# A fused attention, routed expert and feed-forward kernel: routing moved to a score tile's spare columns, first expert tile prepared on GpSimd

## The chip, the cores and the metric

One Trainium2 chip, one core. The metric is device time of one execution in microseconds (us); lower is better. The engines named below are TensorE (PE, with PEld for its weight loads), VectorE (DVE), ScalarE (ACT), GpSimd (POOL) and SyncE (SP), which issues most transfers.

## The reference

Three stages in a row, all in float32:

```python
# 1. attention, (B, H, S, D) = (2, 8, 576, 64)
q_rot, k_rot = rotate(q), rotate(k)
attn = softmax(q_rot @ k_rot.T / sqrt(D));  x = attn @ v      # -> (1152, 512)
# 2. eight experts, top 1
logits = x @ w_gate + modality_bias[modality_id]              # (1152, 8)
e_idx, gate_w = argmax(logits), max(softmax(logits))
out[e_idx == e] = gate_w * (relu(x @ w1[e]) @ w2[e])          # 512 -> 1024 -> 512
# 3. feed forward
h = out @ w_in;  y = (h * tanh(softplus(h))) @ w_out          # 512 -> 2048 -> 512
```

## The kernel before

Every product is made of matmuls on a rounded high part and a low part (value minus high part), so each operand has to be split: a copy to the high part, mostly on ACT, and a subtraction for the low part on DVE or POOL.

**Attention** goes over 16 heads in pairs. For each block of queries PE makes scores (`score`, L930), DVE their maximum (`smax`), ACT the exponential (`sexp`), PE transposes (`tr`), ACT and DVE split the transposed block (`t_hi`, `t_lo`), PE multiplies with v into the tile `avp` (`pv`), ACT copies that out (`f_evac`), PE turns it back and multiplies it with the router's weights in the same matmul (`f_mm`), and DVE divides by the softmax sum (`f_norm`, L1045). `f_norm` writes twice: the 64 columns of a head into `X`, the 8 logits of a head into `LG`. POOL prepares each head's q, k and v ahead of it (L884 to L925) and adds 1e-9 to the softmax sums (`f_rec`).

The order of the whole stage is worked out when the program is built, by `Plan` (L74): each operation has an engine, an estimated time, a key (about when it is due) and the operations it depends on; an engine takes the first operation by key that is ready within 0.05 us, else the one that is ready first. The result is a fixed order on each engine's queue, and an instruction at the head of a queue that is not ready in fact holds up all behind it. Streams (`Plan.add`) are generators whose steps are fitted in between. A step of an engine named in `low` is taken only into a gap that it fits.

**Routing** (`routing`, L307) is done once for each half of the tokens (b = 0 after head 7, b = 1 after head 15): logits, argmax, one matmul that counts tokens for each expert (L362, L363), the row of each token in a sorted scratch buffer, five indirect DMAs from POOL that scatter the rows of `X` there (L413), and a table of which expert and which 304 rows make each expert tile. The intermediates lie in PSUM in `rtile`, which for b = 0 is columns 320 to 511 of `avp`, the bank into which `pv` multiplies. Dependencies are kept tile by tile, so DVE's routing instructions and PE's `pv` wait for each other though they touch other columns.

**The expert stage** has two tiles for each half (`moe_tile`): (0,0), (0,1), (1,0), (1,1). A tile loads its rows (`load_rows`, L571), multiplies them by the gate (`moe_g`, L633, ACT), transposes them (`moe_x`, L650), and takes eight weight chunks (`load_chunk`, `split_chunk`, L588 and L593): four for the first layer, f = 0 to 7, two each, and four for the second, d = 0 to 3. For (0,0) the low parts of chunks 3 and 4 are made on DVE. After the half-0 table, SP reads the tile's registers (`tile_rows`), loads rows and two chunks, and ACT and POOL split these chunks in gaps of the last heads. PE's transposes of (0,0) come behind the attention's last matmul. Then the routing of half 1 runs on DVE, and `pump` puts as many PE steps of the expert tiles before each DVE step as `P["rq"]` says (0.45, 0.47, 0.2 us). Behind it stand nine more PE steps and then `n_extra = nc.values_load(nx)`, a register read on every engine of a value that the last routing instruction (L544) writes: PE cannot go on before it. The scatters of half 1 and the row loads of half 0 touch one scratch buffer, so whichever comes second waits for the other.

**The last stage** (from about 293 us) decodes the feed-forward weights on DVE and runs the two products.

Of the kernel before, what the change touches and what calls it, by code (L numbers as in the profile page):

```python
# [28 lines left out]
XC = DM  # L29
# [39 lines left out]

LOW = ("act", "dve", "pool")  # L70
# [3 lines left out]
class Plan:  # L74
# [72 lines left out]
    def add(self, gen, ready, low=(), end=None):  # L147
        st = {"gen": gen, "ready": ready, "low": low, "end": end}
        st["next"] = next(gen, None)
        self.streams.append(st)  # L150
# [18 lines left out]
    def run(self):  # L169
# [3 lines left out]
        while any(self.todo.values()):  # L173
            best = None
            for e in self.todo:
# [10 lines left out]
                for st in self.streams:  # L186
                    if st["next"][0] != e:
                        continue
                    t = self.start(st)
                    if c is None or t + (st["next"][1] - P["slack"] if e in st["low"] else 0.0) <= c[0]:  # L190
                        c = (t, 0, st)
# [19 lines left out]
def moe_kernel(ctx: ExitStack, tc: tile.TileContext, aps, out):  # L211
# [16 lines left out]
    LG = [xp.tile([128, 5, H, NE], F32, name=f"LG{b}") for b in range(B)]  # L228
# [76 lines left out]
    scat, nxs, tes, tms = [], [], [], []  # L305

    def routing(b, bank):  # L307
# [4 lines left out]
        def near(sh, nm):  # L312
# [19 lines left out]
            out=lg, in_=LG[b].rearrange("p j h e -> p j e h"),  # L332
# [12 lines left out]
        val = near(sh, "val")  # L345
# [27 lines left out]
        if side:  # L373
            V.memset(base[:, 0:1], 0.0)
        yield "dve", 0.2, True
        if side:
            scan()
            room[0] = 90
            pz = near([128, n], "pz")
            V.tensor_tensor(out=pz, in0=ps[:, n:2 * n], in1=base[:, 0:n], op=ALU.add)  # L380
            V.tensor_copy(cnt[:, 0:n], ps[:, 0:n])
        else:
            V.tensor_copy(cnt, ps[:, 0:2 * n])
        sm8 = near([128, 5], "sm8")
        yield "dve", 0.12, True
        V.tensor_reduce(out=sm8, in_=ex, axis=AX.X, op=ALU.add)
        yield "dve", 0.12, True
        V.tensor_scalar(out=sm8, in0=sm8, scalar1=1e-9, scalar2=None, op0=ALU.add)
        yield "dve", 0.12, True
        V.reciprocal(out=X[b][:, :, XC + 1], in_=sm8)  # L390
        if not side:
            yield "dve", 0.12, True
            V.memset(base[:, 0:1], 0.0)
            yield "dve", 0.12, True
            scan()
        if not side:
            pz = t([128, n], "pz")
            yield "dve", 0.12, True
            V.tensor_tensor(out=pz, in0=cnt[:, n:2 * n], in1=base[:, 0:n], op=ALU.add)
        yield "dve", 0.12, True  # L400
# [68 lines left out]
        if side:  # L469
            room[0] = 0  # L470
# [95 lines left out]
    def load_rows(k):  # L566
# [3 lines left out]
        for i, (r0, rn) in enumerate(TCH):  # L570
            ld = nc.sync.dma_start(out=t[:rn, i], in_=scratch[ds(r["c"] + r0, rn), :])  # L571
            if k != "x":
                after_scatters(ld)
# [1030 lines left out]
```

## Time and profile before

| | us |
|---|---|
| median of three runs | 524.64 |
| lowest, highest | 520.6, 524.78 |
| the profiled execution | 524.0 |
| its span, first to last instruction | 522.3 |

| engine | busy us of the span | share |
|---|---|---|
| PE | 481.5 | 92% |
| DVE | 408.8 | 78% |
| POOL | 365.1 | 70% |
| ACT | 332.8 | 64% |

The mean granted clock of PE is 0.98. Matmuls overlap in the profile, so PE counts as busy also where it is not at its best rate; the number of matmuls in a stretch says more. Attention ends near 177 us, the expert stage near 293 us.

### The profile page before, as it was taken

How to read it: one execution, taken by the hardware profiler on the slowest of the kernel's cores; microseconds unless marked ns; L12 is line 12 of the kernel's file. 1: busy time of each engine (PE TensorE's matmuls, PEld its weight loads, DVE VectorE, ACT ScalarE, POOL GpSimd, SP SyncE). 2: the span in 40 equal slices, each digit the busy share in tenths (PEclk: the TensorE clock that was granted, in tenths of full speed). 3: DMA queues.
4: the chain of work that ended last, by engine and by line, in shares of the span. 5: the costliest groups of instructions: out<-in, count | busy, mean ns of one | idle time of the engine just before them, and what ended most of it. 6: DMA issues, size and time to landing. Idle time of an engine off the chain costs nothing.

```text
span 522.3 us, 9180 instructions
## 1 busy us (share of the span) xinstructions
PE 481.5 (92%) x3152; PEld 445.3 (85%) x3152; DVE 408.8 (78%) x622; ACT 332.8 (64%) x748; POOL 365.1 (70%) x359
## 2 busy tenths in 40 slices
PE   2699999998899879998999988899999899999995
PEld 1689999987799778997999987688999789999894
DVE  6478989888989583852467999999999967877773
ACT  2378788766688745454464475666666568776773
POOL 4869999989680535774867566677777558977664
PEclk9969999999999998999999999999999899999999
DMA  6568885866654277594776522022220000100001
GB/s 210 144 160 213 230 226 146 208 191 187 166 107 133 80 266 279 216 315 163 246 249 215 228 82 80 2 80 82 81 82 1 1 1 40 41 21 1 2 2 80
DMA packets 24132, 68.67 MB, mean 131 GB/s; under 512 B 5522, under 2 KB 9810, under 8 KB 22034
## 3 DMA queue, kind: packets, MB, share of 16 engines
q1 hardware_dynamic: 21794, 62.70, 39.7%
q0 software_dynamic: 1456, 4.74, 2.4%
q10 hardware_dynamic: 832, 0.61, 0.4%
q8 instruction: 26, 0.43, 0.3%
q14 instruction: 24, 0.20, 0.1%
HBM read 48.77 MB, written 5.99 MB: 105 GB/s over the span
## 4 chain that ended last, share of the span: by engine, by line
PE 35%; DVE 13%; issue 2%; ACT 2%; POOL 0%; POOLq 0%
PE h L1411 13%; PE o L1468 13%; PE mm L684 9%; DVE ta L1433 6%; DVE yl L1359 2%; DVE wc L1259 2%; DVE wc L1264 1%; DVE ta L1434 1%; DVE wc L1254 1%; ACT w2h L1394 0%; PE mm L650 0%; POOL out_dram L1478 0%; ACT ta L1423 0%; POOLq L1600 0%; ACT ta L1422 0%
## 5 line engine op out<-in xcount | busy, mean ns | idle before, releaser
L1433 DVE RECIPROCAL ta<-ta 128x320 f32<-128x320 f32 (+1 forms) x64 | 124.7, 1948 | 21.9 <-ACT ta L1426 19.7
L1451 POOL TENSOR_TENSOR g<-ta,g 128x320 fp32r<-128x320 f32 (+1 forms) x63 | 60.1, 954 | 61.4 <-issue 29.0
L1468 PE MATMUL o<-w2h,g 128*128 128x512 f32 x288 | 100.4, 396 | 0.0
L1395 POOL TENSOR_TENSOR w2l<-wc,w2h 128x512 fp32r<-128x512 f32 x64 | 85.9, 1364 | 3.4 <-ACT w2h L1394 3.4
L1411 PE MATMUL h<-yh,w2h 128*128 128x320 f32 (+1 forms) x256 | 76.8, 300 | 6.2 <-DVE ta L1434 6.2
L1411 PE MATMUL h<-yl,w2h 128*128 128x320 f32 (+1 forms) x256 | 76.3, 298 | 1.1 <-DVE yl L1359 1.1
L1411 PE MATMUL h<-yh,w2l 128*128 128x320 f32 (+1 forms) x256 | 76.5, 299 | 0.0
L939 PE MATMUL sc<-sk,sq 128*128 128x288 f32 (+1 forms) x320 | 60.7, 322 | 15.1 <-ACT sk L870 9.3
L956 ACT ACTIVATE pexp<-sc,nm 128x576 f32<-128x576 f32 x72 | 53.3, 740 | 23.5 <-DVE nm L949 17.9
L989 ACT ACTIVATE ph<-pt 128x512 fp32r<-128x512 f32 (+2 forms) x112 | 54.5, 509 | 16.8 <-PE pt L969 15.8
L949 DVE TENSOR_REDUCE nm<-sc 128x1 f32<-128x576 f32 x72 | 53.6, 751 | 12.8 <-PE sc L939 11.2
L1468 PEld LDWEIGHTS o<-w2h,g 128*128 128x128 f32 x288 | 54.1, 189 | 11.0 <-POOL g L1451 1.1
L939 PEld LDWEIGHTS sc<-sk,sq 128*128 128x128 f32 (+1 forms) x320 | 48.7, 198 | 17.0 <-ACT sk L870 9.3
L1411 PEld LDWEIGHTS h<-yh,w2h 128*128 128x128 f32 x256 | 48.6, 190 | 11.1 <-DVE ta L1434 7.8
L969 PE MATMUL pt<-ident,pexp 128*128 128x128 f32 (+1 forms) x360 | 55.7, 282 | 2.1 <-DVE rs L1034 1.6
L1468 PE MATMUL o<-w2l,g 128*128 128x512 f32 x144 | 56.8, 394 | 0.0
L1010 PE MATMUL av<-ph,vhl 128*128 128x256 f32 (+1 forms) x160 | 52.0, 340 | 2.4 <-DVE av L331 0.5
L1445 ACT ACTIVATE g<-ta 128x320 fp32r<-128x320 f32 (+1 forms) x64 | 27.9, 436 | 41.3 <-DVE ta L1434 41.2
L995 DVE TENSOR_TENSOR pl<-pt,ph 128x512 fp32r<-128x512 f32 (+1 forms) x80 | 49.3, 629 | 3.2 <-ACT ph L989 2.5
L1411 PEld LDWEIGHTS h<-yl,w2h 128*128 128x128 f32 x256 | 48.6, 190 | 3.6 <-DVE yl L1359 1.4
L1411 PEld LDWEIGHTS h<-yh,w2l 128*128 128x128 f32 x256 | 48.7, 190 | 0.1
L969 PEld LDWEIGHTS pt<-ident,pexp 128*128 128x128 f32 (+1 forms) x360 | 43.9, 141 | 4.0 <-issue 2.1
(445 smaller groups left out, 1222.1 us busy)
## 6 DMA issues: line engine op xcount, KB each, us to landing
wr<-in_wio_dram SPq DMA_DIRECT2D x16, 1024.0 KB, 5.0
xs<-in_qk_dram SPq DMA_DIRECT2D x15, 576.0 KB, 5.3
sk<-ab SPq DMA_DIRECT2D x30, 288.0 KB, 3.8
sq<-ab SPq DMA_DIRECT2D x30, 144.0 KB, 2.3
vraw<-in_v_dram SPq DMA_DIRECT2D x16, 160.0 KB, 3.9
scratch<-zero SPq DMA_DIRECT2D x12, 96.8 KB, 4.4
tabs<-in_rope_dram SPq DMA_DIRECT2D x2, 288.0 KB, 4.8
xs<-in_qk_dram ACTq DMA_DIRECT2D x2, 288.0 KB, 4.5
```

The source lines that it names most:

```text
L939: nc.tensor.matmul(t[:m, hf, :NC2], lhsT=sq[:, c:c + m], rhs=sk[:, z, hf * NC2:(hf + 1) * NC2], start=(z == 0), stop=(z == 1),)
L949: nc.vector.tensor_reduce(out=nm[n, j], in_=sc[n, j][:, :, :NC2], axis=AX.XY, op=ALU.max, negate=True)
L956: nc.scalar.activation(out=pe, in_=sc.pop((n, j))[:, :, :NC2], func=AF.Exp, bias=nm.pop((n, j)), accum_out=st[n, hf][:, i:i + 1],)
L969: nc.tensor.transpose(out=t[:kn, o:o + 128], in_=pexp[n, j][:, k0:k0 + kn], identity=ident)
L989: nc.scalar.activation(out=block(ph, n, hf, kts, slice(0, kn)), in_=psum(n, hf, kts, kn), func=AF.Copy)
L995: nc.vector.tensor_tensor(out=block(pl, n, hf, kts, slice(0, 128)) if kn == 128 else block(ph, n, hf, kts, slice(64, 128)), in0=psum(n, hf ...
L1010: nc.tensor.matmul(av[n, hf][:, :u.nq], lhsT=vhl[n][:, kt].rearrange("p a d -> p (a d)"), rhs=src[:, kt, u.at:u.at + u.nq], start=(kt == 0 ...
L1395: nc.gpsimd.tensor_tensor(out=lo[:, cs], in0=w[:, cs], in1=hi[:, cs].bitcast(F32), op=ALU.subtract)
L1411: nc.tensor.matmul(ps[:, :w], lhsT=wt[:, c], rhs=m[g, i][:, c], start=(n == 0), stop=(n == 11))
L1433: nc.vector.reciprocal(out=ta, in_=ta)
L1451: eng.tensor_tensor(out=gt[q][1][:, o:o + w], in0=tas.pop((q, i))[:, :w], in1=gt[q][0][:, o:o + w].bitcast(F32), op=ALU.subtract,)
L1468: nc.tensor.matmul(acc[g, t], lhsT=a[:, s], rhs=b, start=(f == 0 and z == 0), stop=(f == FC2 - 1 and z == 2),)
```

## The change

1. `X` takes the logits too: a head has 72 columns in it (`XC = H * XW`), `LG` is gone, and `f_norm` writes once. Scattered rows and loaded rows are 580 columns wide instead of 516.
2. The score tiles become two fixed tiles `scp`. The routing of half 0 keeps its first intermediates in the spare columns of one of them, and a gate (`is_spare`) lets its steps be placed only between that tile's maximum and its next scores. The part behind the counting matmul works in the matmul's own bank and in SBUF, in one step; 1e-9 is added on ACT.
3. The scatters of half 0 become a stream that takes only gaps on POOL. The table of half 0 becomes a stream of its own, in SBUF, that starts after the last head's low part (`plo`) on POOL. Rows are loaded when both are done.
4. Scatters of one half no longer wait for row loads of the other, nor the loads for them.
5. For tile (0,0) POOL makes the gates and the high and low parts of chunks 0 to 2, as soon as the rows are there; PE's transposes become twelve matmuls in four operations `xt` of the plan, due at key `XK` = 162, with ACT and DVE splitting them. Softmax sums of the last two heads go to ACT.

```diff
-XC = DM
+XC = H * XW
+XK = 10.0 * B * H + 2.0
...
-    LG = [xp.tile([128, 5, H, NE], F32, name=f"LG{b}") for b in range(B)]
...
-        if side:
-            scan()
-            room[0] = 90
-            pz = near([128, n], "pz")
+        yield "dve", 0.8, True
+        V.tensor_tensor_scan(
+            out=base[:, 1:], data0=ps[:, 0:n], data1=zero[:, :n],
+            initial=0.0, op0=ALU.add, op1=ALU.add,
+        )
+        pz = ps[:, 2 * n:3 * n]
...
-        V.tensor_scalar(out=sm8, in0=sm8, scalar1=1e-9, scalar2=None, op0=ALU.add)
+        yield "act", 0.2, True
+        nc.scalar.activation(out=sm8, in_=sm8, func=AF.Copy, bias=1e-9)
...
+        if b:
+            yield from scatters()
+        else:
+            cur["scatters"] = scatters()
+            yield "mark", 0.0, False
+            side = False
...
-    def after_scatters(ld):
-        for o in scat:
+    def after_scatters(ld, b):
+        for o in scat[1 - b]:
+            tc.declare_no_dep(ld.ins, o, reason="rows of the other half")
+        for o in scat[b]:
...
-        yield "act", 0.95, False
-        nc.scalar.activation(out=hi, in_=w, func=AF.Copy)
+        if k == (0, 0) and i < 3:
+            yield "pool", 1.3, False
+            nc.gpsimd.tensor_scalar(
+                out=hi, in0=w, scalar1=1.0, scalar2=0.0, op0=ALU.mult, op1=ALU.add
+            )
...
-            yield "act", 0.5, i == 2
+            yield ("pool", 0.7, False) if k == (0, 0) else ("act", 0.5, i == 2)
...
+        def is_spare(t):
+            return spare[0] == 1 or spare[0] == 2 and t >= spare[1]
...
-            for dst, c0, c1 in (
-                (X[b][:, j0:j0 + m, h * D:(h + 1) * D], 0, D),
-                (LG[b][:, j0:j0 + m, h], D, XW),
-            ):
+            nc.vector.tensor_tensor(
+                out=X[b][:, j0:j0 + m, h * XW:(h + 1) * XW], in0=x[:, :m],
+                in1=r[:, :m, None].to_broadcast([128, m, XW]), op=ALU.mult,
+            )
...
+    def ahead(done):
+        yield from feed.loads(5)
+        yield from moe_g(k0)
+        x_new(k0)
+        done()
+        yield from feed.splits(3)
...
+        for c in range(KC):
+            op = lambda n, e, d, fn, dep, **kw: plan.op((n, c), e, d, XK, fn, deps=dep, **kw)
+            op("xt", "pe", 0.35, lambda c=c: xt(c), ["gate0"], take=[("ring", ("x", c))])
+            op("xh", "act", 0.4, lambda c=c: x_hi(k0, c, xps[c]), [("xt", c)])
+            op("xl", "dve", 0.44, lambda c=c: x_lo(k0, c, xps[c]), [("xh", c)],
+               give=[("ring", ("x", c))])
...
-            plan.add(until_pe(gen0), plan.now + 2.2, low=LOW)
+            plan.add(begin, plan.now + 2.2, low=("act", "dve"))
...
+        plan.op("scatter", "sp", 0.0, z, scatter, deps=["rt_row"])
+        plan.op("table", "sp", 0.0, z, table, deps=["rt_row", ("plo", B * H - 1)])
         plan.op(
             "rows", "sp", 2.2, z, weights,
-            deps=["rt_end", ("stack", B * H - 1), ("vload", B * H - 1)],
+            deps=["rt_end", "rt_sc", ("stack", B * H - 1), ("vload", B * H - 1)],
         )
```

## Rows read from the trace of the kernel before

**Rows 1.** Stretches of attention: length, busy (x instructions) per engine, clock, DMA, GB/s.

```profile
80.00:100.00 20.00, 20.00 (x163) 19.53 (x162) 17.91 (x40) 16.32 (x43) 18.86 (x21) 1.00 0.68 175
100.00:120.00 20.00, 18.61 (x138) 16.54 (x137) 16.36 (x49) 13.47 (x34) 17.34 (x22) 1.00 0.72 196
120.00:140.00 20.00, 16.09 (x115) 13.92 (x114) 17.44 (x50) 12.34 (x32) 17.78 (x22) 1.00 0.70 186
140.00:160.00 20.00, 19.96 (x159) 19.13 (x159) 18.01 (x42) 16.16 (x41) 11.69 (x15) 1.00 0.49 105
```

**Rows 2.** Waits between 100 and 140 us: total us, times, longest.

```profile
ACT pexp L956 <- DVE base L374: 1.7, 1, 1.7
...
PEld av L1010 <- DVE av L331: 0.8, 1, 0.8
```

**Rows 3.** Timeline of POOL: start, us, line, operation, [idle before <-releaser].

```profile
111.60 1.42 POOL L890 TENSOR_TENSOR xs<-xs 128x576 f32<-128x576 f32 x1
114.15 1.20 POOL L413 DMA_INDIRECT scratch<-X,row  x1 [1.12 <-DVE row L410]
...
120.85 0.67 POOL L896 TENSOR_SCALAR ab<-xs 128x576 fp32r<-128x576 f32 x1
...
134.14 2.65 POOL L884 TENSOR_TENSOR xs<-xs,tabs 128x1152 f32<-128x1152 f32 x1
...
150.86 1.42 POOL L905 TENSOR_TENSOR ab<-xs,ab 128x576 fp32r<-128x576 f32 x1
...
180.44 2.37 POOL L593 TENSOR_TENSOR wlo(0, 0)_2_2682<-wraw(0, 0)_2_2554,whi(0, 0)_2_2680 128x1024 fp32r<-128x1024 f32 x1 [3.36 <-ACT whi(0, 0)_2_2680 L588]
190.33 1.08 POOL L413 DMA_INDIRECT scratch<-X,row  x1 [7.52 <-DMA xrow(0, 1)_2757<-scratch]
```

**Rows 4.** Timeline of DVE, the same columns.

```profile
134.40 2.41 DVE L519 CAST tbl<-te 1x4 int32<-1x4 f32 x1
...
176.91 0.29 DVE L1054 TENSOR_TENSOR X<-xo,rs 128x128 f32<-128x128 f32 x1 [1.80 <-PE xo L1040]
...
177.77 0.47 DVE L657 TENSOR_TENSOR xl(0, 0)_2605<-mm,xh(0, 0)_2604 128x304 fp32r<-128x304 f32 x1 [0.49 <-ACT xh(0, 0)_2604 L655]
...
187.46 0.15 DVE L410 TENSOR_SCALAR row<-rt 128x5 int32<-128x5 f32 x1
...
195.35 0.14 DVE L544 TENSOR_TENSOR nxi<-nx,nx 1x1 int32<-1x1 f32 x1
```

**Rows 5.** Timeline of PE from the end of attention.

```profile
176.20 0.67 PE L1040 MATMUL xo<-mov,avt 128*128 128x72 f32 x4 [0.47 <-ACT avt L1019]
176.70 2.24 PE L650 MATMUL mm<-ident,xrow(0, 0)_2385 128*128 128x128 f32 x12
...
181.39 0.41 PE L362 MATMUL mm<-oh,ones 128*128 128x40 f32 x2 [0.69 <-DVE base L374]
...
192.64 0.30 PE L684 MATMUL mm<-xl(0, 0)_2605,whi(0, 0)_3_2734 128*128 128x304 f32 x1
192.78 0.30 PE L684 MATMUL mm<-xh(0, 0)_2604,wlo(0, 0)_3_2736 128*128 128x304 f32 x1
196.38 0.38 PE L684 MATMUL mm<-xh(0, 0)_2604,whi(0, 0)_3_2734 128*128 128x304 f32 x1 [3.29 <-DVE hl(0, 0)_2677 L709]
```

**Rows 6.** Stretches behind that wait, columns as in rows 1.

```profile
196.00:200.00 4.00, 3.62 (x19) 3.65 (x20) 2.02 (x3) 0.42 (x1) 2.92 (x3) 0.73 0.73 220
200.00:204.00 4.00, 4.00 (x27) 4.00 (x25) 0.74 (x1) 2.33 (x4) 1.19 (x1) 0.85 0.98 393
```

**Rows 7.** SP's register reads of the table (ns min/median/max), and its row loads.

```profile
L549 SPq TENSOR_LOAD <-tbl x4: 271/509/981, 154.1 to 195.6; - x4
...
158.32 1.48 SPq L571 DMA_DIRECT2D xrow(0, 0)_2385<-scratch  x3
```

**Rows 8.** Landing of the last row load of tile (0,0), us.

```profile
xrow(0, 0)_2385<-scratch SPq DMA_DIRECT2D x1, 96.8 KB, 3.6
```

**Rows 9.** POOL's one-input form: busy us, mean ns, idle before.

```profile
L896 POOL TENSOR_SCALAR ab<-xs 128x576 fp32r<-128x576 f32 x15 | 10.1, 674 | 2.0 <-DMA sk<-ab 1.1
```

More of the change, by code (lines that the diff above doesn't have):

```diff
@@ L145, in take, with add @@
                 self.slots[r].append(end + LAT[o[3]])
-    def add(self, gen, ready, low=(), end=None):
-        st = {"gen": gen, "ready": ready, "low": low, "end": end}
+    def add(self, gen, ready, low=(), end=None, gate=None):
+        st = {"gen": gen, "ready": ready, "low": low, "end": end, "gate": gate}
         st["next"] = next(gen, None)
@@ L189, in run @@
                     t = self.start(st)
+                    if st["gate"] and not st["gate"](t):
+                        continue
                     if c is None or t + (st["next"][1] - P["slack"] if e in st["low"] else 0.0) <= c[0]:
@@ L410, in routing, with scatters @@
         V.tensor_scalar(out=row, in0=pos, scalar1=s1, scalar2=o1, op0=ALU.mult, op1=ALU.add)
[L411 to L420 removed]
+        def scatters():
+            for j, (_, qn) in enumerate(QT):
+                yield "pool", 1.07, False
+                sc = nc.gpsimd.indirect_dma_start(
+                    out=scratch,
+                    out_offset=bass.IndirectOffsetOnAxis(ap=row[:qn, j:j + 1], axis=0),
+                    in_=X[b][:qn, j], in_offset=None,
+                )
+                for o in scat[0] + scat[1]:
+                    tc.declare_no_dep(sc.ins, o, reason="every token has a row of its own")
+                for o in early if b else ():
+                    tc.declare_no_dep(sc.ins, o, reason="rows of the other half")
+                scat[b].append(sc.ins)
+                nc.gpsimd.memset(spacer, 0.0)
+        if b:
[4 more added lines that the diff above has]
+            side = False
+        room[0] = 256
         ce = near([1, NE], "ce")
@@ L468, in routing @@
         s8 = [1, ns, NE]
[L469 to L470 removed]
+        room[0] = 0
         lt = near(s8, "lt")
@@ L1197, in hook, with until_mark, mark @@
         cur["rbank"] = lambda: bank("counts")
+        def until_mark():
+            for y in r0:
+                if y[0] == "mark":
+                    return
+                yield y
+        def mark(name):
+            return lambda t: plan.done.update({name: ("dve", t)})
         def start():
-            plan.add(until_pe(r0), plan.now, end=lambda t: plan.done.update(rt=("dve", t)))
+            plan.add(until_pe(r0), plan.now, end=mark("rt"), gate=cur["spare"])
         def rest():
             next(r0)
-            plan.add(r0, plan.now + 0.2, end=lambda t: plan.done.update(rt_end=("dve", t)))
+            plan.add(until_mark(), plan.now + 0.8, end=mark("rt_row"))
@@ new lines, in scatter, with table, xt @@
+        def scatter():
+            plan.add(cur["scatters"], plan.now, low=("pool",), end=mark("rt_sc"))
+        def table():
+            plan.add(r0, plan.now, end=mark("rt_end"))
+        begin = ahead(lambda: plan.done.update(gate0=("pool", plan.free["pool"])))
+        cur["begin"] = begin
+        xps = {}
+        def xt(c):
+            xps[c] = bank(f"x{c}")
+            x_tr(k0, c, xps[c])
+        for c in range(KC):
[4 more added lines that the diff above has]
+               give=[("ring", ("x", c))])
```

149 lines of the change are left out of this document (82 added, 67 removed).

## The prediction

> **What bounds the kernel now.** I read first the busy times by stretch of the attention [rows 1]. Where no routing runs, PE is busy throughout and gets 163 matmuls through in 20 us, 8.15 in a microsecond, while DVE and POOL are near 90%. From 100 to 140 us it does 138 and 115. At the former rate these 253 need 31.0 us: routing half 0 inside the attention costs 9.0 us, 3.1 of them up to 120 and 5.9 behind. The waits of that stretch say how [rows 2]: ACT's exponential stood 1.7 us for a routing instruction on DVE, and PE's product stood for the router's reduction into the bank they share. POOL's timeline shows another part [rows 3]: between the addition at 111.60 and the next preparation at 120.85 it only scatters (about 1.3 us a piece, five of them), so later heads' operands come some 7 us late.
>
> Then I read the timelines around the end of attention. PE goes from the last outputs (176.20) to twelve transposes of tile (0,0) (2.2 us) and its products [rows 5]; it waits 0.69 us for the argmax and stops at 192.92, until 196.38. The wait is put down to DVE, but the product at 196.38 needs nothing new: the instruction behind the nine steps is the register read of `nx`, which DVE writes at 195.49 [rows 4]. So DVE's routing chain, from the norm at 176.91 to 195.49 (18.6 us), sets this point, and the read takes 0.9 more. Behind the stop the granted clock falls to 0.73 and 0.85 of a stretch of 4 us [rows 6], between its levels of 1.2 and 2.4 GHz: 1.1 + 0.6 = 1.7 us lost. From there on the stages follow one another; I take a shift at this point to reach the end.
>
> **Routing half 0 (the gain).** The sum is made against the profiled execution, 524.0 us, 0.6 under the median. Of the 9.0 us the false waits on `avp` go, and the scatters no longer come before the heads' preparation. What stays is DVE's work: in the first part some 15 instructions, in the table some 18 of 0.15 us upward [rows 4], about 0.2 with their issue, 3.6 in all, into an engine busy 18.0 of 20 [rows 1]. Half of the first part's loss stays (1.5), and the table costs 2.0 where it now lies (from 147 us), the rest fitting into DVE's idle tenth: gain 9.0 - 3.5 = 5.5. Bounds: 9.0 if all of this is hidden; 9.0 - 3.1 - 3.6 = 2.3 if the first part stays and the table is paid whole. I take 5.5, since PE is the full engine in [rows 1]. One write instead of two in `f_norm` shortens DVE; PE's full rate hides it, so nothing. Wider rows: PE, DVE and ACT touch no more than before; transfers have slack, nothing.
>
> **Gates, chunks and transposes.** Price of a chunk on POOL: its low part 2.37 [rows 3], its high part at 0.674 for 576 columns [rows 9] 1.2 for 1024: 3.57. When do they start? The table starts behind the last `plo`, now 152.3 [rows 3], then 5.5 earlier, 146.8. Its 18 instructions alternate with attention's (18.0 us for 42 instructions, 0.43 each [rows 1]): 18 x 0.63 = 11.3, end at 158.1. SP's register reads take 4.2 (154.1 to 158.32), three row loads 1.5 [rows 7], the last lands 3.6 later [rows 8], its gate takes about 0.7: 168.1. Attention's PE work would end at 176.87 - 5.5 = 171.4, so gates are done 3.3 us before it. Chunks are ready at 171.7, 175.2 and 178.8; PE, starting near 173.6 and taking 3.3 us for each, needs them at 174, 177 and 180.6: hidden by some 2 us. If the rows are 2 us later, that cover is gone.
>
> The twelve transposes cost PE 2.2 us wherever they stand. In the attention they fill waits at its end such as the 0.47 before 176.20 [rows 5]; I let them hide 1.0 and cost 1.2. But the planner counts 2.2 us for the register reads and nothing for the landing, so it believes the gates done 4.3 us after the table, and not 10. It may put a transpose up to 5.7 us too early on PE's queue, and everything of the last head's `tr`, `pv` and `f_mm` is behind it. I take 1.0 for this (bounds 0 and 5). Transposes: 2.2 inside the attention.
>
> **From the last outputs to the register read.** Now 176.20 to 196.38, 20.2 us, with twelve transposes and 90 products. After: DVE's chain is rid of four `xl` of 0.42 (1.7, [rows 4]), one addition (0.2) and about 1.0 of waiting for a PE that starts its products sooner, and has a detour over ACT (0.4): 18.6 - 2.5 = 16.1, and with the read (0.9) and the 0.7 ahead of the norm 17.7. DVE steps fall from 42 to 39, so the pump puts about 6 products more before the read, worth 6 x 0.14 = 0.8 (0.14 is the step between products in [rows 5]). Gain 20.2 - 17.7 + 0.8 = 3.3. PE needs 0.3 + 96 x 0.14 + 0.7 = 14.4 us of the 17.7, so 2.6 us of stop remain of 3.5, and I give the clock's 1.7 half back: 0.8 (bounds 0 and 1.7). Scatters of half 1 start when their rows are known (187.6, [rows 4]) and not when a row load has landed (190.33 [rows 3], 2.7 later); that only lets weight loads keep pace. Since PE comes sooner to chunks 6 and 7, I charge 0.5 for weights that arrive just in time.
>
> Sum: -5.5 + 2.2 - 3.3 - 0.8 + 0.5 = -6.9: 517.1, against the median 517.7. I say 517.5.
>
> **A rule against it.** DVE's cast of four numbers took 2.41 us, from 134.40 to 136.81, just until POOL's multiplication of 134.14 to 136.79 was through [rows 3, 4]; both work in SBUF. The Trainium skill, "GPSIMD Engine Reference", Key points, says that POOL shares its SBUF interfaces with DVE and contends with DVE instructions in a two-port mode or with two SBUF inputs; the row agrees. By the rule the sum would be 522, by the one row it stays at 517. The change moves the table from PSUM to SBUF, which is the form that was held; its price from rows is below.
>
> **The rivals.**
>
> *Forecast*, 517.5 (512 to 519.3), chance 0.52.
>
> *Transposes wait at the head of PE's queue* (the other side). If the planner also thinks the table done in 18 x 0.25 = 4.5 us instead of 11.3, PE can stand at `xt` for up to 5.7 + 6.8 = 12.5 us. For: nothing in the planner knows of the landing, and 0.05 us of a gap are enough for it. Against: PE shows no wait from 140 to 160 [rows 1], and the key makes them late. Without this wait the sum gives -7.9, with the clock's 0.8 lost again -7.1 and another 1.7 for a second fall -5.4: from 5.4 us of standing it is a loss. At 5, 523.6 (chance 0.15); at 12.5, 524.0 - 5.4 + 12.5 = 531.1 (chance 0.12).
>
> *The waits only move* (the change doesn't do what it says). A routing step between a score tile's maximum and its next scores can hold exponential and scores as it held `pv`. For: 1.7 us of ACT's exponential behind a routing step in [rows 2]. Against: the gate keeps PE's writes out of that window, and only eight steps use it. Gain 2.3 instead of 5.5: 520.3; chance 0.13.
>
> *The table is held by POOL.* Each of 18 SBUF instructions can wait as the cast did, but only while POOL works: five scatters (6.7 us, [rows 3]) and the last head's v, about 1.3. So at most 8.0 us later: gates at 176.1, past attention's end; first chunk 179.7, products 0.8 later than now (178.9), yet the routing chain starts sooner and the stop at the read is gone: some 2 us of gain left, 522; chance 0.08.
>
> **How the numbers follow.** About 1% is what a measurement of this kernel can tell from no change: 519.4 and 529.9 bound it. Forecast, a part of the second case and of the third below that mark: faster 0.57. Standing of 5 us, the rest of the waits that move, the held table: same 0.31. Standing for 12.5: slower 0.12. The range starts at the best case, gain 9.0, no standing, clock whole: 524.0 - 9.0 + 1.2 - 3.3 - 1.7 + 0.5 = 511.7, and reaches past the held table and PE's standing of 5 to 524; the 12 in 100 above and a few below are left out.
>
> **What would show it.** Right: some 160 matmuls in 20 us all through 100 to 140; no wait of DVE for `av`; five scatters in POOL's gaps near 146 to 153; row loads of (0,0) on SP near 162; gates and three chunks on POOL from 165 to 179; transposes before the last outputs with no wait over 1 us; PE's last outputs near 173; the register read passed near 190; scatters of half 1 without a wait for a row load. Wrong: a wait of PE at an `xt`; row loads later than 166; PE waiting for chunk 1 or 2; a fall of the clock before 175; a rate under 7 between 100 and 140; a stop at the register read as long as before.

## The result and the profile after

| | median us | runs |
|---|---|---|
| kernel before | 523.91 | 16 |
| changed kernel | 527.20 | 16 |

The ratio is 1.0076, with a 95% interval of 1.0051 to 1.0101: the change costs about 4 us. The forecast was 517.5 us with a range up to 524; the sign was wrong, and the time lies outside the range. The profiled execution of the changed kernel took 524.2 us with a span of 522.0, and before's span was 522.3, so these two profiles alone hide the loss.

They differ in something that is no part of the change. Between 20 and 40 us PE's granted clock is not the same in every execution, even of kernels that are alike up to there, and the end of attention moves with it. In before's profile it was 0.74 there, with 97 matmuls; in that of the changed kernel it was 0.91, with 117. Experiment `e2_tied` below is the changed kernel in all that bears on the attention, and its profile began as before's did. Windows of before (columns as in [rows 1]):

```profile
20.00:40.00 20.00, 16.94 (x97) 15.79 (x98) 11.74 (x24) 10.99 (x27) 14.26 (x17) 0.74 0.77 191
```

The same of `e2_tied`:

```profile
20.00:40.00 20.00, 16.93 (x97) 15.71 (x97) 11.79 (x24) 11.13 (x28) 14.41 (x17) 0.74 0.75 189
100.00:120.00 20.00, 18.82 (x151) 17.95 (x150) 18.54 (x46) 14.42 (x38) 18.94 (x21) 1.00 0.81 198
120.00:140.00 20.00, 19.06 (x150) 17.92 (x149) 17.05 (x37) 15.51 (x40) 18.21 (x20) 1.00 0.68 176
```

With this like start its last outputs came at 173.13 us and in `e4_decode` at 173.88, against 176.20 in [rows 5]. The attention is 2.3 to 3.1 us shorter, not the 6.2 that the two first profiles show (2.0 to 3.4 with `e7_before_decode` and `e9_psum_pump`, which start alike too). The stretches that routing slowed down [rows 1] now do 151 and 150 matmuls instead of 138 and 115. At the 8.15 matmuls in a microsecond of [rows 1] these 48 more are worth 5.9 us, an estimate; so some 3 us of that are lost again between 140 us and the last outputs, where the table and the transposes now stand.

What follows is read from the changed kernel's own profile. The count product is the matmul that counts tokens for each expert. `hl` is the low part of the first layer's output, which DVE makes. The merge is the last part of the routing: it joins the tables of both halves and writes `nxi`, the value of the register read. Windows, first attention, then behind the first and around the second of PE's two long stops (compare [rows 1] and [rows 6]):

```profile
100.00:120.00 20.00, 18.59 (x147) 17.68 (x147) 19.20 (x49) 14.88 (x40) 18.93 (x20) 1.00 0.80 211
120.00:140.00 20.00, 19.69 (x158) 18.75 (x156) 17.12 (x38) 16.09 (x42) 17.88 (x22) 1.00 0.68 161
178.00:182.00 4.00, 4.00 (x20) 4.00 (x19) 1.82 (x10) 0.63 (x2) 0.49 (x1) 0.57 0.94 373
192.00:196.00 4.00, 1.06 (x4) 1.09 (x5) 3.35 (x10) 0.36 (x1) 1.16 (x1) 0.50 0.69 238
196.00:200.00 4.00, 4.00 (x23) 4.00 (x22) 1.08 (x1) 0.00 (x0) 0.00 (x0) 0.69 0.93 330
```

PE at the last outputs, at the count product, and at the first product behind the register read (compare [rows 5]):

```profile
169.98 0.67 PE L1099 MATMUL xo<-mov,avt 128*128 128x72 f32 x4 [0.47 <-ACT avt L1075]
...
176.88 0.41 PE L369 MATMUL mm<-oh,ones 128*128 128x40 f32 x2 [2.85 <-DVE base L380]
...
194.94 0.59 PE L723 MATMUL mm<-hh(0, 0)_2582,whi(0, 0)_4_2695 128*128 128x304 f32 x1 [5.82 <-DVE hl(0, 0)_2583 L748]
```

DVE ahead of the count product, and from the end of the table to `nxi` (compare [rows 4]):

```profile
172.85 0.47 DVE L748 SCALAR_TENSOR_TENSOR hl(0, 0)_2583<-mm,hh(0, 0)_2582 128x304 fp32r<-128x304 f32 x1 [0.56 <-ACT hh(0, 0)_2582 L746]
...
174.52 0.47 DVE L748 SCALAR_TENSOR_TENSOR hl(0, 0)_2583<-mm,hh(0, 0)_2582 128x304 fp32r<-128x304 f32 x1 [0.36 <-ACT hh(0, 0)_2582 L746]
175.46 1.23 DVE L610 TENSOR_TENSOR wlo(0, 0)_3_2626<-wraw(0, 0)_3_2430,whi(0, 0)_3_2624 128x1024 fp32r<-128x1024 f32 x1 [0.47 <-ACT whi(0, 0)_3_2624 L605]
176.60 0.22 DVE L364 TENSOR_TENSOR oh<-iota,rt 128x40 f32<-128x40 f32 x1
...
189.69 0.14 DVE L525 CAST tbl<-rt 1x4 int32<-1x4 f32 x1
189.76 3.43 DVE L534 TENSOR_SCALAR mm<-iotat,nx 1x8 f32<-1x8 f32 x1
193.11 0.15 DVE L539 TENSOR_TENSOR md<-te,rt 1x16 f32<-1x16 f32 x1
...
194.05 0.14 DVE L550 TENSOR_TENSOR nxi<-nx,nx 1x1 int32<-1x1 f32 x1
```

POOL: the gates of tile (0,0), and two low parts (compare [rows 3]):

```profile
155.58 4.66 POOL L651 TENSOR_SCALAR xrow(0, 0)_2307<-xrow(0, 0)_2307 128x512 f32<-128x512 f32 x3 [7.67 <-DMA xrow(0, 0)_2307<-scratch]
...
188.50 2.36 POOL L610 TENSOR_TENSOR wlo(0, 0)_5_2755<-wraw(0, 0)_5_2693,whi(0, 0)_5_2753 128x1024 fp32r<-128x1024 f32 x1
190.81 2.35 POOL L610 TENSOR_TENSOR wlo(0, 0)_6_2853<-wraw(0, 0)_6_2751,whi(0, 0)_6_2851 128x1024 fp32r<-128x1024 f32 x1
```

DVE where the last stage begins:

```profile
304.89 2.15 DVE L1533 RECIPROCAL ta<-ta 128x320 f32<-128x320 f32 x1 [0.63 <-ACT ta L1526]
...
309.66 0.49 DVE L1534 SCALAR_TENSOR_TENSOR ta<-ta,h 128x320 f32<-128x320 f32 x1
310.06 1.30 DVE L1364 SCALAR_TENSOR_TENSOR wc<-wr,wc 128x1024 int32<-128x1024 int32 x1
311.29 2.14 DVE L1533 RECIPROCAL ta<-ta 128x320 f32<-128x320 f32 x1
```

PE doesn't wait for the moved transposes: the gates are done at 160.2 us, and its two long waits are others. From the last outputs to the count product it takes 6.90 us (before 5.19), with a stop of 2.85: DVE has two `hl` and chunk 3's low part (1.23 us) in front of the argmax. From the count product to the register read it takes 18.06 us (before 14.99), with a stop of 5.82. The `hl` that this row names is no operand of the product: as in the kernel before, PE stands at the register read, which is through 0.75 us behind the end of `nxi`. And `nxi` is late because one DVE instruction on eight numbers took 3.43 us, from 189.76 to 193.19, and POOL's two low parts ended at 193.16; the same instruction took 0.21 us in the kernel before, while POOL scattered (L528 is its line there):

```profile
194.55 0.21 DVE L528 TENSOR_SCALAR mm<-iotat,nx 1x8 f32<-1x8 f32 x1
```

PE's clock was 0.57 of full speed from 178 to 182, behind the first stop; around the second it was 0.5 from 192 to 196 and 0.69 up to 200, and fell further than in [rows 6]. And in the last stage a decode step (1.30 us at 310.06; a step is a third of the decoding of one weight chunk) stands between reciprocals.

So that kernels can be compared whatever their start, the profiles are cut at five events: the last outputs (the last `xo` matmul), the count product, PE's first product behind the register read, DVE's first reciprocal, and the end of the span. All in us, from the profile of each; "first 20" is the number of PE's matmuls from 20 to 40 us.

| kernel | ratio to before (95%) | first 20 | last outputs at | to count | to read | to reciprocal | to end |
|---|---|---|---|---|---|---|---|
| before | 1 | 97 | 176.20 | 5.19 | 14.99 | 111.62 | 214.3 |
| changed | 1.0076 (1.0051 to 1.0101) | 117 | 169.98 | 6.90 | 18.06 | 109.95 | 217.1 |
| e1_merge_psum | 0.9973 (0.9936 to 1.0010) | 120 | 170.31 | 6.91 | 15.12 | 110.97 | 215.6 |
| e2_tied | 1.0071 (1.0040 to 1.0102) | 97 | 173.13 | 6.90 | 18.06 | 112.91 | 217.5 |
| e3_low3_pool | 0.9944 (0.9908 to 0.9980) | 125 | 170.71 | 5.20 | 14.26 | 109.47 | 217.5 |
| e4_decode | 1.0002 (0.9974 to 1.0029) | 97 | 173.88 | 6.89 | 18.54 | 110.87 | 214.3 |
| e5_all | 0.9898 (0.9853 to 0.9944) | 108 | 171.52 | 5.20 | 13.89 | 111.84 | 214.7 |
| e6_pump | 0.9904 (0.9866 to 0.9943) | 107 | 171.24 | 3.67 | 17.30 | 112.91 | 212.8 |
| e7_before_decode | 1.0022 (0.9994 to 1.0050) | 98 | 175.91 | 5.18 | 14.89 | 115.99 | 213.5 |
| e8_tr_behind | 0.9955 (0.9921 to 0.9990) | 107 | 170.75 | 5.01 | 14.93 | 114.76 | 215.1 |
| e9_psum_pump | 0.9961 (0.9929 to 0.9994) | 99 | 172.84 | 3.67 | 15.51 | 114.43 | 214.3 |
| e10_psum_pump_low3 | 0.9957 (0.9921 to 0.9993) | 107 | 172.04 | 3.68 | 15.78 | 111.43 | 213.8 |
| e11_act | 1.0122 (1.0078 to 1.0165) | 108 | 172.11 | 9.26 | 18.19 | 109.69 | 217.2 |
| e12_one_input | 1.0022 (0.9984 to 1.0060) | 125 | 169.91 | 6.91 | 19.33 | 110.06 | 215.9 |

In `e10_psum_pump_low3` PE does not stop at the read; its row takes the product at which `e9_psum_pump` stops.

Against the kernel before, with a like start (`e2_tied`; `e4_decode` but for its last column): attention -2.3 to -3.1, to the count product +1.7, to the read +3.1 to +3.6, to the reciprocal -0.8 to +1.3, to the end +3.2. That makes 6.2 for `e2_tied` and 5.4 for `e4_decode` with the other's last column; the ratio over all runs says 4.0, with 2.7 to 5.3 in its interval.

### The profile page after: what moved, and what is told of

The parts are those of the page before. It is cut to its first block, busy times and chain, and to the rows that moved or that the text cites. A ratio compares the mean times of both kernels' runs of the same rounds, so it can differ in the third digit from the quotient of the medians.

```text
span 522.0 us, 9087 instructions
## 1 busy us (share of the span) xinstructions
PE 478.6 (92%) x3152; PEld 441.7 (85%) x3152; DVE 402.7 (77%) x586; ACT 327.3 (63%) x749; POOL 377.1 (72%) x360
## 4 chain that ended last, share of the span: by engine, by line
PE 28%; DVE 18%; issue 4%; DMA 2%; ACT 1%; POOL 0%; SPq 0%; POOLq 0%; ACTq 0%
DVE ta L1533 11%; PE h L1511 10%; PE o L1568 10%; PE mm L723 7%; DVE wc L1359 2%; DMA wraw(1, 0)_6_3627<-in_w_dram 2%; DVE ta L1534 1%; DVE wc L1364 1%; DVE yl L1459 1%; DVE wc L1354 1%; PE mm L672 0%; POOL out_dram L1578 0%; SPq L582 0%; POOLq L1700 0%; ACT xrow(1, 1)_3608 L657 0%
## 5 line engine op out<-in xcount | busy, mean ns | idle before, releaser
L1551 POOL TENSOR_TENSOR g<-ta,g 128x320 fp32r<-128x320 f32 (+1 forms) x63 | 57.5, 913 | 63.7 <-issue 33.3
L1495 POOL TENSOR_TENSOR w2l<-wc,w2h 128x512 fp32r<-128x512 f32 x64 | 88.8, 1409 | 3.3 <-ACT w2h L1494 3.3
L991 PE MATMUL sc<-sk,sq 128*128 128x288 f32 (+1 forms) x320 | 59.5, 319 | 15.1 <-ACT sk L918 9.3
L991 PEld LDWEIGHTS sc<-sk,sq 128*128 128x128 f32 (+1 forms) x320 | 47.5, 194 | 17.2 <-ACT sk L918 9.3
L1025 PEld LDWEIGHTS pt<-ident,pexp 128*128 128x128 f32 (+1 forms) x360 | 42.1, 138 | 4.9 <-issue 1.1
```

The costliest lines, as they stand in the source:

```text
L991: nc.tensor.matmul(t[:m, hf, :NC2], lhsT=sq[:, c:c + m], rhs=sk[:, z, hf * NC2:(hf + 1) * NC2], start=(z == 0), stop=(z == 1),)
L1025: nc.tensor.transpose(out=t[:kn, o:o + 128], in_=pexp[n, j][:, k0:k0 + kn], identity=ident)
L1495: nc.gpsimd.tensor_tensor(out=lo[:, cs], in0=w[:, cs], in1=hi[:, cs].bitcast(F32), op=ALU.subtract)
L1551: eng.tensor_tensor(out=gt[q][1][:, o:o + w], in0=tas.pop((q, i))[:, :w], in1=gt[q][0][:, o:o + w].bitcast(F32), op=ALU.subtract,)
```

## The experiments

The first theory had three losses behind a real gain: DVE's own queue ahead of the argmax, DVE held by POOL at the merge, and a decode step too many in the stage that DVE bounds.

**Merge with an operand in PSUM.**

```diff
-        m = rp.tile([1, n0], F32, tag="mm", name="mm")
+        m = cur["rtile"][0:1, 400:400 + n0]
...
-            out=tes[1][:, 2:2 + n0], in0=tms[1][:, 2:2 + n0], in1=d, op=ALU.add
+            out=tms[1][:, 2:2 + n0], in0=tms[1][:, 2:2 + n0], in1=d, op=ALU.add
...
-        V.tensor_copy(ei, tes[1][:, 2:])
+        V.tensor_copy(ei, tms[1][:, 2:])
...
-        V.tensor_tensor(out=nx, in0=nxs[0], in1=nxs[1], op=ALU.add)
+        V.scalar_tensor_tensor(out=nx, in0=cur["qi"][:, NE - 1:NE], scalar=-2.0, in1=nxs[0], op0=ALU.add, op1=ALU.add)
```

> The changed kernel, in which the merge of the two tables and the sum behind it read or write one operand in PSUM, so that no DVE instruction between the table's end and nxi has all its operands in SBUF. Theory (the chain from the last norm to the register read sets the time here, and the 3.43 us of the merge's first instruction is DVE held by POOL's two low parts): that instruction takes about 0.2 us although POOL still works from 188.5 to 193.2 us; nxi is written near 190.9 instead of 194.05, PE passes the register read near 191.7 instead of 194.94, and the time falls by 3 us or a little more (the clock's fall behind the read gets shorter too): some 524, ratio to the kernel before 0.997 to 1.002. Rival 1 (DVE was not held by POOL; the instruction waited for something else): it still ends when POOL's low parts end, and the time stays at 527. Rival 2 (the read is passed early, but the stages behind it are set by weight loads or by DVE's work): read near 191.7, first reciprocal of the last stage earlier by under 1 us, ratio 1.005 or more.

DVE in this kernel (`rt` is the tile in PSUM), and then POOL:

```profile
190.24 0.22 DVE L534 TENSOR_SCALAR rt<-iotat,nx 1x8 f32<-1x8 f32 x1
...
191.35 0.18 DVE L548 CAST ei<-rt 1x32 int32<-1x32 f32 x1
191.46 0.14 DVE L550 SCALAR_TENSOR_TENSOR nxi<-rt,nx 1x1 int32<-1x1 f32 x1
```

```profile
188.86 2.37 POOL L610 TENSOR_TENSOR wlo(0, 0)_5_2755<-wraw(0, 0)_5_2693,whi(0, 0)_5_2753 128x1024 fp32r<-128x1024 f32 x1
191.18 2.37 POOL L610 TENSOR_TENSOR wlo(0, 0)_6_2852<-wraw(0, 0)_6_2751,whi(0, 0)_6_2850 128x1024 fp32r<-128x1024 f32 x1
```

The merge's first instruction took 0.22 us and the cast 0.18, under the same POOL work. The stretch to the read fell from 18.06 to 15.12 us, the ratio to 0.9973. DVE was held by POOL, and the read is on the path; both rivals fall.

**Scatters tied again.**

```diff
-                for o in early if b else ():
-                    tc.declare_no_dep(sc.ins, o, reason="rows of the other half")
```

> The changed kernel, in which the scatters of half 1 are ordered again behind the row loads of half 0 that came before them, as in the kernel before. Theory (untied scatters let POOL's low parts of chunks 5 and 6 fall on the merge): scatters start near 187 to 190 us instead of 181.50, the merge's first instruction takes 0.2 instead of 3.43 us because POOL only scatters then, and PE passes the register read near 191.7 instead of 194.94; but the low part of chunk 5 then comes near 196 to 198, so that PE waits for it behind the first nine products of section d: the time ends within 2 us of the changed kernel's 527, ratio 1.004 to 1.010. Rival (the early scatters are a gain by themselves): the low part of chunk 5 is late by so much that the time is over 2 us longer than the changed kernel's, ratio over 1.011.

Both expectations missed the point: the ratio lies in the range of the first, but not for its reason. POOL in this kernel:

```profile
185.08 1.03 POOL L409 DMA_INDIRECT scratch<-X,row  x1 [11.25 <-DVE rt L429]
```

The first scatter still waits for DVE alone, 5.05 us behind the count product (4.62 in the changed kernel), so the row loads of (0,1) have landed by then (the last was issued by 176.3 and took 4.2). Time and stretches are those of the changed kernel: untying the scatters of half 1 is worth nothing here, and costs nothing.

**Low part of chunk 3 on POOL.**

```diff
-P = {'sd': (3, 4), ...
+P = {'sd': (4,), ...
```

> The changed kernel, in which the low part of chunk 3 is made by POOL and not by DVE. Theory (PE's wait of 2.85 us for the count product is DVE's own queue: two hl and this low part of 1.23 us ahead of the argmax): the wait shrinks to 1.2 to 1.7 us, the clock does not fall at 178 us, DVE's chain is shorter by 1.2 us plus what the clock no longer takes, the register read is passed 1 to 3 us earlier, and the time falls by as much: some 525, ratio 1.001 to 1.005. Rival (the chain is set behind it, by the hold of the merge until POOL has done chunk 6): the merge's first instruction ends at 193 us as before and the time stays within 0.7 us of the changed kernel's, ratio 1.006 to 1.009.

PE in this kernel:

```profile
175.91 0.42 PE L369 MATMUL mm<-oh,ones 128*128 128x40 f32 x2 [1.16 <-DVE base L380]
...
190.17 0.59 PE L723 MATMUL mm<-hh(0, 0)_2582,whi(0, 0)_4_2695 128*128 128x304 f32 x1 [3.52 <-DVE hl(0, 0)_2583 L748]
```

DVE:

```profile
187.26 1.13 DVE L534 TENSOR_SCALAR mm<-iotat,nx 1x8 f32<-1x8 f32 x1
```

The stop at the count product is 1.16 us instead of 2.85. The gain, 1.3%, is over twice what was expected, because the low parts of chunks 5 and 6 now fall otherwise (186.01 to 188.37, and 192.01): the merge's first instruction takes 1.13 us and not 3.43, so this one edit takes most of the second loss too.

**One decode step more before the last stage**, in the changed kernel and, as a control, in the kernel before.

```diff
-'dec': (8, 8, 8)
+'dec': (8, 8, 7)
```

> The changed kernel, in which one decode step comes at every 21 and not at every 24 products in the last routed tile, so that as many are done before the first reciprocal as in the kernel before. Theory (2.9 us earlier at the start of the last stage shrink to 0.3 at its end because DVE bounds that stage and has one decode step of about 1.2 us more in it): no decode step stands behind a reciprocal, the time falls by 1 to 2 us, ratio 1.003 to 1.006. Rival (the gain is lost there for another reason, such as PE's clock at the end): ratio unchanged at 1.0076 within 0.0015.

> The kernel before, with a decode step at every 21 and not at every 24 products in the last routed tile. Theory (the kernel before has no decode step behind a reciprocal, the changed one has one, so that this edit takes back a loss of the change and is no gain by itself): first reciprocal to the end stays at 214.3 us, ratio 0.998 to 1.002. Rival (the edit is a gain in either kernel, and the changed kernel lost nothing there): first reciprocal to the end shorter by 2 to 3 us, ratio 0.993 to 0.996.

In the changed kernel the edit takes 2.8 us off the last stretch (217.1 to 214.3, before's own figure) and brings the ratio to 1.0002. In the kernel before it is no gain (1.0022): what the last stretch gains (0.8) the one ahead of it loses (4.4, in one execution that was 2.4 us above its median). There the added step came ahead of a `yl`, a low part of the last stage's input, and PE stood for that:

```profile
309.56 0.64 PE L1411 MATMUL h<-yl,w2h 128*128 128x320 f32 x1 [2.85 <-DVE yl L1359]
```

So the decode step was lost by the change. Counted over all profiles: of 48 steps 22 stand behind the first reciprocal in the changed kernel and the five variants of it that leave this as it is (`e1_merge_psum`, `e2_tied`, `e3_low3_pool`, `e11_act`, `e12_one_input`), and their last stretch is 215.6 to 217.5 us; in the kernel before and the other variants of the changed one it is 21 steps and 212.8 to 215.1. The reason is in the pump: decode steps are dealt out one to 24 PE steps of the part behind the merge, and the changed kernel has fewer of those steps, as more products are done in the pump.

`e4_decode` shows the hold a second time, as it differs from the changed kernel only from tile (1,1) on. DVE, then POOL:

```profile
195.18 0.21 DVE L534 TENSOR_SCALAR mm<-iotat,nx 1x8 f32<-1x8 f32 x1
...
196.16 2.35 DVE L548 CAST ei<-te 1x32 int32<-1x32 f32 x1
```

```profile
192.72 2.39 POOL L610 TENSOR_TENSOR wlo(0, 0)_5_2755<-wraw(0, 0)_5_2693,whi(0, 0)_5_2753 128x1024 fp32r<-128x1024 f32 x1
196.12 2.35 POOL L610 TENSOR_TENSOR wlo(0, 0)_6_2853<-wraw(0, 0)_6_2751,whi(0, 0)_6_2851 128x1024 fp32r<-128x1024 f32 x1 [1.02 <-ACT whi(0, 0)_6_2851 L605]
```

Here POOL had a gap from 195.11 to 196.12, and the merge's first instruction met it: 0.21 us. The cast behind it met chunk 6's low part and took 2.35, until that was done.

**All three edits together.**

> The changed kernel with the three edits together that were made one at a time: the merge reads or writes PSUM, the low part of chunk 3 is on POOL, and a decode step comes at every 21 products in the last routed tile. Theory (three separate losses behind the attention: DVE's own queue ahead of the argmax, DVE held by POOL at the merge, one decode step too many in the stage that DVE bounds): PE's wait for the count product 1.2 us, merge steps 0.2 us each, last outputs to register read 18.5 to 19.5 us, first reciprocal to the end near 214.3 instead of 217.1; ratio to the kernel before 0.984 to 0.990. Rival (the three take the same time away, so that they don't add): ratio 0.992 or more.

0.9898: 19.1 us from the last outputs to the read, and a last stretch of 214.7. The three don't add (their single gains make 3.1%, together 1.8%), as `e1_merge_psum` and `e3_low3_pool` remove much of the same hold. It beats both kernels.

**Fewer products ahead of the argmax**, and the same number in all before the read.

```diff
-'vl': 9, ... 'rq': (0.45, 0.47, 0.2)
+'vl': 27, ... 'rq': (0.17, 0.47, 0.2)
```

> The changed kernel, in which a routing step ahead of the count product lets PE have 0.17 us of products and not 0.45 (some 10 products before the count product instead of 28), and the 18 that this takes away stand behind the merge, ahead of the register read. The low part of chunk 3 stays on DVE, but behind the argmax. Theory (the transposes used to take 2.2 us of what a step owes PE; without them products and with them hl and chunk 3's split come ahead of the argmax): from the last outputs to the count product 3.8 to 4.5 us instead of 6.9, PE's wait there about 1.9, the register read passed 2 to 4 us earlier, ratio to the kernel before 0.998 to 1.003. Rival 1 (only the place of the products in PE's queue is changed, and the merge's hold by POOL ends as late as before): from the last outputs to the read still 24 us or more, ratio 1.006 or more. Rival 2 (fewer products beside the chain: PE stops longer and its clock falls for longer): ratio over 1.010.

The count product came 3.67 us behind the last outputs, with 9 products in front of it in the trace (24 in the changed kernel, 11 in the kernel before). It gained 1.7%, more than expected: the 18 products behind the merge count for the decode steps again, and the last stretch was 212.8. The merge was still held there (its first instruction took 2.34 us, until the low part of chunk 5 was done), and yet the ratio is that of `e5_all`.

**Transposes behind the attention again**: the `xt`, `xh`, `xl` operations taken out of the plan, and `x_new` out of `ahead`, so that `moe_x` makes them.

> The changed kernel with the twelve transposes of the first tile behind the last outputs again, as in the kernel before; gates and three chunks stay on POOL, routing stays in the score tile. Theory (moved transposes take their 2.2 us inside the attention, and behind it they kept products, hl and chunk 3's split from coming ahead of the argmax): last outputs some 2 us earlier, last outputs to the count product near 5.2 us as in the kernel before with a wait under 1 us, last outputs to the register read 20 to 23 us (the lower end if POOL does not hold the merge), so the read is passed 4 to 7 us earlier than in the changed kernel, ratio to the kernel before 0.994 to 1.001. Rival (the loss lies in gates and chunks on POOL, or in the untied scatters, and not in the transposes): last outputs to the read 24 us or more, ratio 1.006 or more.

5.01 and 14.93, the kernel before's stretches, and 0.9955: with the transposes behind the attention, 7 products stand ahead of the count product and DVE's chunk 3 behind it. Beside `e5_all`, `e6_pump` and `e10_psum_pump_low3`, which start alike, the last outputs come 0.5 to 1.3 us earlier. These three, the same in the attention, are 0.8 us apart themselves, so the twelve transposes cost some 1 us inside the attention, with that uncertainty.

**Both: merge in PSUM and fewer products ahead; and chunk 3's low part on POOL as well.**

> The changed kernel with two edits: the merge reads or writes PSUM, and only some 10 products stand ahead of the count product while 18 move behind the merge (which also gives the steps back by which decode steps are counted). Theory (the hold of DVE and the order ahead of the argmax are two losses that add): last outputs to the count product 3.7 us, count product to the register read 15.0 instead of 17.3, last outputs to the read 18.5 to 19 us; ratio to the kernel before 0.982 to 0.988. Rival (what the read gains is lost behind it to weights or the clock): ratio 0.989 to 0.993.

> The kernel with the merge in PSUM and 10 products ahead of the count product, in which also the low part of chunk 3 is on POOL. Theory (each DVE instruction that leaves the chain between the last norm and the register read shortens it by its length, as long as PE has products beside it): another 1.2 us off the part between the count product and the read, ratio to the kernel before 0.980 to 0.986. Rival (PE's own products and their hl set that part by now, or POOL's scatters wait for this low part and weights come late): the part stays within 0.4 us and the ratio within 0.002 of the one without this edit.

`e9_psum_pump` has nearly the stretches that were expected, 19.2 us from the last outputs to the read, but its ratio (0.9961) lies above both ranges, and beside `e6_pump` (0.9904) the merge in PSUM shows no gain. SP, ACT and PE of `e9_psum_pump`, and a window behind, first of it and then of `e6_pump`:

```profile
193.02 0.34 SPq L551 DMA_DIRECT2D extra<-ei  x1
193.78 0.36 SPq L591 DMA_DIRECT2D wraw(0, 0)_6_2812<-in_w_dram  x1
```

```profile
198.94 1.06 ACT L605 ACTIVATE whi(0, 0)_6_2851<-wraw(0, 0)_6_2812 128x1024 fp32r<-128x1024 f32 x1 [7.62 <-DMA wraw(0, 0)_6_2812<-in_w_dram]
199.90 1.32 ACT L657 ACTIVATE xrow(0, 1)_2679<-xrow(0, 1)_2679 128x512 f32<-128x512 f32 x2
```

```profile
192.02 0.38 PE L723 MATMUL mm<-hh(0, 0)_2582,whi(0, 0)_4_2713 128*128 128x304 f32 x1 [1.16 <-DVE hl(0, 0)_2583 L748]
...
200.66 0.33 PE L672 MATMUL mm<-ident,xrow(0, 1)_2679 128*128 128x128 f32 x1 [1.72 <-ACT xrow(0, 1)_2679 L657]
```

```profile
204.00:220.00 16.00, 16.00 (x105) 16.00 (x105) 10.81 (x12) 7.59 (x14) 11.45 (x5) 0.89 0.47 156
```

```profile
204.00:220.00 16.00, 16.00 (x117) 16.00 (x116) 11.72 (x13) 8.08 (x14) 13.15 (x6) 1.00 0.58 197
```

Chunk 6's load stands on SP behind the register reads of the table and the transfer of `ei`, 20.9 us behind the last outputs; in `e6_pump` it was 21.1 (192.32), though the read came 1.8 us later there, and in `e5_all` 11.9, ahead of the read. ACT's high part of chunk 6 ends at 200.0, the gates of (0,1) queue behind it, and PE stops 1.72 us for them, where `e6_pump`, coming later, stopped 0.23. From 204 to 220 its clock is 0.89 with 105 matmuls, in `e6_pump` 1.00 with 117. So what the read gave was lost again at the weights and by the clock: the first reciprocal comes 133.6 us behind the last outputs, in `e6_pump` 133.9. Why the last stretch is 1.5 us longer than that of `e6_pump`, these rows don't show.

In `e10_psum_pump_low3` (0.9957) the rival holds: the ratio is that of `e9_psum_pump` within 0.002. PE doesn't stop at the read at all, but 1.33 us for chunk 3's low part ahead of it and 1.60 for an `hl` behind. Yet from the last outputs to the end its profile is as short as that of `e5_all` (344.7 and 345.6 us), so why the ratios of these two kernels are worse than `e5_all`'s stays open; the intervals of both overlap with it.

**Gates and high parts on ACT again.**

> The changed kernel with the gates and the high parts of the first three chunks of tile (0,0) on ACT again, as in the kernel before; routing and transposes stay inside the attention. Theory (POOL's part of the change is a small gain: 3 gates of 1.6 us and 3 high parts of 1.04 us lie where POOL had nothing else, while ACT has the last heads' exponentials): ACT's exponentials and the last outputs come later, transposes fall behind the last outputs or PE waits for them, products start 1 to 3 us later, ratio to the kernel before 1.008 to 1.015. Rival (ACT had room for them, and the POOL part is no gain or harms): ratio 1.004 or less.

1.0122 against 1.0076, intervals that overlap: POOL's part of the change is a gain of some half percent or nothing, and not the loss. PE's stop at the count product becomes 5.21 us, since chunk 3's high part comes later on ACT (178.87, behind its load) and its low part is still ahead of the argmax on DVE.

**One-input work of POOL under the merge.**

```diff
+            for _ in range(4 * b):
+                dummy = rp.tile([128, 1024], F32, tag="dum", name="dum")
+                nc.gpsimd.tensor_scalar(
+                    out=dummy.rearrange("p (a c) -> p a c", c=128), in0=ones[:, None].to_broadcast([128, 8, 128]),
+                    scalar1=1.0, scalar2=0.0, op0=ALU.mult, op1=ALU.add,
+                )
```

> The changed kernel, in which POOL makes four additional multiplications of 128x1024 with one input in SBUF (1.04 us each, into a tile that nobody reads) between the scatters of half 1 and the low part of chunk 5, so that the merge on DVE meets one-input and not two-input work of POOL. Theory 1 (only POOL's two-input work holds a DVE instruction with all operands in SBUF): the merge's first instruction takes 0.2 us and nxi is written near 191 us; PE then waits for chunk 5, whose low part ends near 195. Theory 2 (any POOL compute in SBUF holds it): the merge's first instruction ends with the additional ones or with the low parts behind them, 193 us or later. The time itself is some 0 to 4 us longer than the changed kernel's in both.

DVE, then POOL:

```profile
191.02 0.87 DVE L540 TENSOR_SCALAR mm<-iotat,nx 1x8 f32<-1x8 f32 x1
...
191.99 1.02 DVE L547 TENSOR_TENSOR md<-md,mm 1x16 f32<-1x16 f32 x1
...
193.51 1.82 DVE L554 CAST ei<-te 1x32 int32<-1x32 f32 x1
```

```profile
188.55 4.45 POOL L422 TENSOR_SCALAR dum<-ones 128x1024 f32<-128x1024 f32 x4
192.96 2.34 POOL L616 TENSOR_TENSOR wlo(0, 0)_5_2763<-wraw(0, 0)_5_2701,whi(0, 0)_5_2761 128x1024 fp32r<-128x1024 f32 x1
```

Theory 2 holds: three instructions of the merge were held, by 0.7, 0.9 and 1.6 us, the first two by one-input work, though the first was through at 191.9 and not at 193. But each hold ended with one POOL instruction (the four take 1.11 each), where in the changed kernel it went on through two that followed at once. `nxi` came 1.2 us later than in the changed kernel. Both theories had the time up to 4 us longer; it is not longer, and the ratio (1.0022) can't be told from the changed kernel's.

## Why the prediction was wrong

**The attention: right in the sum, by two errors that cancel.** The forecast put the last outputs near 173 us; at a like start they came at 173.1 and 173.9. Its terms were -5.5 for routing and +2.2 for the transposes. The transposes cost some 0.5 to 1.3 (`e8_tr_behind`), so routing gained some 2.8 to 4.4, within the bounds of 2.3 to 9.0. Up to 140 us 5.9 of the 9.0 came back, where the forecast had 7.5. That the sum came out was luck. The planner's missing landing time did no harm: at the like start of `e2_tied` the table ended at 152.8 us and not 158, rows were loaded from 155.8 and not 162, and the gates, done at 163.4, had 5 us to spare before the first transpose at 168.2 (the three gates took 4.7 us, of which the forecast counted 0.7). The rival in which PE stands at `xt` falls by that, and so does the held table.

**From the last outputs to the register read: the step that failed.** The forecast was 17.7 us and -3.3 in the sum; it took 25.0 (-3.3 became +4.8). Two things were missing in it.

It took four `xl` of 0.42 off DVE's chain and counted "about 1.0 of waiting for a PE that starts its products sooner" as a further gain. It did not ask what the pump puts in the transposes' place. Each DVE step owes PE 0.45 us of work; the transposes used to take 2.2 of that. Without them products take it all, 24 in the trace ahead of the count product instead of 11, and products bring two `hl` and the low part of chunk 3 onto DVE ahead of the argmax. `e3_low3_pool`, `e6_pump` and `e8_tr_behind` each take away another link of this and each brings the 6.9 us back to 5.2 or less. This is shown.

The second is the hold. The forecast had the row (a cast of four numbers held 2.41 us by POOL) and the rule, and applied both to the table of half 0 only, where the change moves instructions into SBUF. It did not look at the instructions that stay in SBUF, the merge, for what POOL would do beside them. In [rows 3, 4] POOL was scattering while the merge ran; since the scatters now start 4.6 us behind the count product and not 8.9, POOL was through with them and at low parts. `e1_merge_psum` takes 2.9 us of the 3.1 back. The forecast said of earlier scatters "that only lets weight loads keep pace"; it had what is done earlier, not what comes next on that queue.

**The clock** was to give back 0.8. With stops of 2.85 and 5.82 us it fell twice instead, to means of 0.57 (178 to 182) and 0.5 of full speed (192 to 196).

**"I take a shift at this point to reach the end"** failed as well: 1.3 to 3.2 us are lost in the last stretch in six profiles, by a decode step that no longer fits in front of it. The forecast named 6 products more before the read as a gain of 0.8 and did not see that products are also what decode steps are counted by.

**The weights** (+0.5) and the untied scatters were no loss in the changed kernel; the weights are the next bound once the read is early (`e9_psum_pump`).

Of the rivals none was it. The rule against the change was the nearest: the mechanism was the right one, placed at the wrong instructions, and priced as a delay of the gates where it fell on the path.

## What to carry to other kernels

When work is taken out of a stream that is dealt out by a budget, ask what the budget buys next, and in whose queue that stands; the same for a queue that starts earlier: what will it be doing when the other engine comes. Small instructions on the path with all operands in SBUF should be looked at together with everything POOL may do beside them; moving one operand to PSUM, or the big subtraction to another time, was worth 1% here in the changed kernel, though beside `e6_pump` the first showed no gain: what one wait gives, the next can take. And compare profiles only after cutting them at the same events, since a different start alone moved the end of attention by 3 to 4 us.

## What the runs showed of the hardware

A DVE instruction of 1x8, 1x16 or 1x32 with all operands in SBUF did not end before the POOL instruction beside it did (3.43, 1.02, 2.35 us instead of 0.16 to 0.21); with one operand in PSUM it took 0.14 to 0.22 beside the same POOL work. The Trainium skill, "SBUF — State Buffer", section "Who interferes with whom", says that DVE and GpSimd lock a shared pair of ports for a whole instruction, that casts and scalar forms can take that pair, and that forms with two SBUF inputs contend with a GpSimd instruction that reads SBUF; the traces agree, for POOL work with one input too (0.87 and 1.02 us in `e12_one_input`). The hold of 3.43 us (3.44 in `e2_tied`) went on through two POOL instructions in a row. Those of `e12_one_input` ended with one, and in `e11_act` the same DVE instruction was through after 1.12 us, between the same two low parts. These runs show that and don't explain it.

PE's clock between 20 and 40 us was 0.74, 0.83, 0.91 or 1.00 of full speed in different executions of kernels that are the same up to there. Why it differs stays open.
